# A load order and the transposes of two tiles at the start of a fused attention and MLP kernel: x tile 2 behind w1's third quarter, the transposes one group forward

## The chip, the cores and the metric

One core of a Trainium2 chip. The metric is the device time of one execution in microseconds (us), as a median of several. All runs told of here are of the fast or undisturbed kind; the granted clock of TensorE was 0.999 or 1.000 in every profile. TensorE is called PE, VectorE DVE, ScalarE ACT, GpSimd POOL, and SP is the queue that issues most loads. Tiles of x and groups of matmuls are counted from 0, the quarters of w1 from first to fourth.

## The reference, cut to what matters

The program adds three things: the input, a recurrent attention layer with memory tokens over the normalized input, and a mixer MLP over the normalized input. The first stage of the MLP:

```python
def _B_ref(x, w1, w2, w3, w4):        # x is already layernormed once
    h = _gelu(_layernorm(x, axis=-1) @ w1)      # x: 2048 x 1024, w1: 1024 x 1024
    # ... shifts by one and two tokens, w2, residual, second layernorm, w3, w4 ...
```

x is 2048 tokens of 1024 values, taken in 16 tiles of 128 tokens. w1 is 1024 x 1024.

## The kernel before

The whole kernel takes some 1510 us and PE is busy nearly all of them. The first 30 us are the start of the MLP: load x tiles and w1, normalize each tile (DVE and POOL), transpose it on PE against an identity, copy the transposed tile from PSUM to SBUF (ACT), multiply by w1 (PE), apply GELU (ACT). The loads are issued in this order on one queue:

```python
load_x(0)
for c in range(4):                     # w1 in four quarters of 512 KB
    nc.sync.dma_start(w1_sb[:, 2 * c:2 * c + 2, :], w1_v[:, 2 * c:2 * c + 2, :])
    if c < 2:
        load_x(1 + c)                  # an x tile is 256 KB
for n in range(3, 7):
    load_x(n)
# ... w2 in four parts, then load_x(7) to load_x(9) ...
```

The first tile is multiplied row block by row block, so that it can begin with the first quarter. The transposes of tile 1 stand ahead of the last two row blocks, which are the fourth quarter:

```python
def stage1_k(xn2T):
    # ...
    for k in range(KT):                # KT = 8; quarter c is k = 2c and 2c + 1
        if k == KT - 2:
            tr(1, 0)                   # four transposes each
            tr(1, 1)
        for co in range(KT):
            nc.tensor.matmul(pss[co // 4][:, co % 4, :], w1_sb[:, k, co * P:(co + 1) * P], xn2T[:, 0, k, :], # ...
```

Tiles 1 to 3 are multiplied group by group (eight output blocks `co`, each a group of eight matmuls over k). The transposes of the next tile lie between the groups that `between` names:

```python
def stage1(n0, nt, xn2T, between, j0=0):
    for co in range(KT):
        # ... eight matmuls, then GELU on ACT ...
        for f in between.get(co, ()):
            f()

for n in range(1, NPE):
    # ... statistics and normalization of tiles n and n + 1 on DVE ...
    if n == 1:
        stage1_k(tiles2[0])
    elif n < 4:
        stage1(n - 1, 1, tiles2[(n - 1) // 2 * 2], {7 - n: [lambda n=n: tr(n, 0)], 8 - n: [lambda n=n: tr(n, 1)]}, (n - 1) % 2)
```

Of the kernel before, what the change touches and what calls it, by code (L numbers as in the profile page):

```python
# [77 lines left out]
def kernel(  # L78
# [115 lines left out]
    with tc.manual_schedule(engines={mybir.EngineType.PE, mybir.EngineType.SP, mybir.EngineType.Pool}), ExitStack() as actx:  # L194
# [6 lines left out]
        with ExitStack() as bctx:  # L201
# [13 lines left out]
            with ExitStack() as hctx:  # L215
# [7 lines left out]
                with ExitStack() as p0:  # L223
# [7 lines left out]
                    def load_x(n):  # L231
                        if n < NT:
                            xts[n] = ring.tile([P, D], BF16, tag="xt", bufs=10, name=f"xt{n}")
                            nc.sync.dma_start(xts[n][:], x_v[:, n, :])

                    load_x(0)
                    for c in range(4):
                        nc.sync.dma_start(w1_sb[:, 2 * c:2 * c + 2, :], w1_v[:, 2 * c:2 * c + 2, :])
                        if c < 2:
                            load_x(1 + c)  # L240
                    for n in range(3, 7):
                        load_x(n)
                    for i in range(4):
# [6 lines left out]
                    def norm_stats(n, part=None):  # L250

                        if n >= NT:
                            return
                        xt = xts[n]
                        if n not in stats:
                            stats[n] = [ring.tile(shape, F32, tag=tag, bufs=6, name=f"{tag}{n}") for tag, shape in (("st", [P, 2, 6]), ("mv", [P, 2]), ("ab", [P, 2]), ("rr", [P, 2]), ("nm2", [P, 1]))]
                        st, mv, ab, rr, nm2 = stats[n]
                        if part in (None, 0):
                            nc.vector.bn_stats(st[:, 0, :], xt[:, 0:512])
                        if part == 0:  # L260
                            return
                        nc.vector.bn_stats(st[:, 1, :], xt[:, 512:1024])
                        nc.vector.bn_aggr(mv[:], st[:])
                        nc.vector.scalar_tensor_tensor(ab[:], epsm[:], mv[:, 1:2], epsa[:], op0=ALU.mult, op1=ALU.add)
                        nc.gpsimd.tensor_tensor(rr[:], ab[:], neghalf[:], op=ALU.pow)
                        if n >= NPE:
                            nc.gpsimd.tensor_scalar(nm2[:], mv[:, 0:1], rr[:, 1:2], -1.0, op0=ALU.mult, op1=ALU.mult)
# [12 lines left out]
                    def norm1(n):  # L280
                        st, mv, ab, rr, nm2 = stats[n]
                        xn = xn_keep[n // 4][:, n % 4]
                        nc.vector.tensor_scalar(xn, xts[n][:], mv[:, 0:1], rr[:, 0:1], op0=ALU.subtract, op1=ALU.mult)
                        nc.gpsimd.dma_start(xn_v[:, n, :], xn)
                        load_x(n + 10)
                        if n in (12, 15):
                            load_w3()
                        return xn

                    def transposes(xn2, xn2T, jj, half, halves=False):  # L290
                        ps = psum0.tile([P, 4, P], F32, tag="tr")
                        for k in range(4):
                            nc.tensor.matmul(ps[:, k, :], xn2[:, (half * 4 + k) * P:(half * 4 + k + 1) * P], ident[:], start=True, stop=True)
                        step = 2 if halves else 4
                        for i in range(0, 4, step):
                            nc.scalar.copy(xn2T[:, jj, half * 4 + i:half * 4 + i + step, :], ps[:, i:i + step])

                    def stage1_k(xn2T):

                        pss = [psum.tile([P, 4, P], F32, tag="mm", bufs=4, name=f"ps{i}") for i in range(2)]  # L300
                        for k in range(KT):
                            if k == KT - 2:
                                tr(1, 0)
                                tr(1, 1)
                            for co in range(KT):
                                nc.tensor.matmul(pss[co // 4][:, co % 4, :], w1_sb[:, k, co * P:(co + 1) * P], xn2T[:, 0, k, :],
                                                 start=(k == 0 and co % 4 == 0), stop=(k == KT - 1), skip_group_check=True)
                        for i in range(2):
                            nc.scalar.activation(hTB[:, 4 * i:4 * i + 4, 2:2 + P], pss[i][:], ACTF.Gelu_apprx_tanh)

                    def stage1(n0, nt, xn2T, between, j0=0):
                        w = nt * P
                        for co in range(KT):
                            ps = psum.tile([P, 512], F32, tag="mm", bufs=4)
                            for k in range(KT):
                                nc.tensor.matmul(ps[:, :w].rearrange("p (n t) -> p n t", t=P), w1_sb[:, k, co * P:(co + 1) * P],  # L316
                                                 xn2T[:, j0:j0 + nt, k, :], start=(k == 0), stop=(k == KT - 1))
                            nc.scalar.activation(hTB[:, co, 2 + n0 * P:2 + n0 * P + w], ps[:, :w], ACTF.Gelu_apprx_tanh)
                            for f in between.get(co, ()):
                                f()  # L320
# [13 lines left out]
                    tiles2, xn2s = {}, {}  # L334

                    def norm2_of(n):
                        if n % 2 == 0:
                            tiles2[n] = xn2T_tile()
                        xn2s[n] = norm2(n, tiles2[n - n % 2], n % 2)

                    def tr(n, half, halves=False):
                        transposes(xn2s[n], tiles2[n - n % 2], n % 2, half, halves)
# [9 lines left out]
                    for n in range(1, NPE):  # L352
                        if n > 1:
                            norm_stats(n + 1, 0)
                        norm2_of(n)
                        norm_stats(n + 1, 1 if n > 1 else None)
                        if n > 1:
                            norm1(n - 2)
                        if n == 1:
                            stage1_k(tiles2[0])  # L360
                        elif n < 4:
                            stage1(n - 1, 1, tiles2[(n - 1) // 2 * 2], {7 - n: [lambda n=n: tr(n, 0)], 8 - n: [lambda n=n: tr(n, 1)]}, (n - 1) % 2)
                    stage1(3, 1, tiles2[2], {0: [lambda: tr(4, 0)], 2: [lambda: tr(4, 1)], 4: [lambda: tr(5, 0)], 5: [lambda: tr(5, 1)]}, 1)

                    def prep(n):
# [44 lines left out]
            with ExitStack() as p3:  # L410
# [118 lines left out]
                for tb in range(4):  # L529
# [18 lines left out]
                    for j in range(4):  # L548
                        n = tb * 4 + j
# [462 lines left out]
```

## Time and profile before

| | before |
|---|---|
| median of the first three runs | 1510.9 us (1510.87 to 1511.14) |
| span of the profile | 1509.0 us |
| PE busy | 1499.1 us |
| w1's second, third, fourth quarter landed | 7.69, 9.67, 11.03 |
| PE starts the sixteen matmuls of the third and of the fourth quarter | 9.715, 11.08 |
| first transposes of tile 6, called **M** below | 26.40 |

How to read it: a time without a unit is us from the first instruction of the profiled execution. A transfer has landed when the last of its sixteen landing marks is in the trace (the profile counts 16 DMA engines). M is a milestone: all PE work of the changed stretch lies before it. "The last sixteen" are the matmuls of the first tile with w1's fourth quarter. The distance from the last sixteen to M tells what the moved transposes do, and the distance from the fourth quarter's landing to the last sixteen tells what the moved load does; in the profiles of the table further below neither depends on how late the loads were in one execution. The lines of this profile stand in the prediction.

### The profile page before, as it was taken

The numbers are of one execution on the slowest core, as the hardware profiler recorded it, in microseconds if no ns is written. First come the engines' busy times: TensorE is split into PE (matmuls) and PEld (weight loads), VectorE is DVE, ScalarE is ACT, GpSimd is POOL, SyncE is SP. The second block draws the span as 40 slices with busy tenths as digits, with TensorE's granted clock in tenths as the row PEclk, the third lists the DMA queues.
The fourth block names the chain that finished last, engine by engine and source line by source line (L and its number), as shares of the span: only waits on it lengthen the run. The fifth ranks groups of instructions, "written<-read, shape, count | busy, mean of one in ns | idle before, by whom it ended". The sixth has DMA issues, their size and how long they took to land.

```text
span 1509.0 us, 24273 instructions
## 1 busy us (share of the span) xinstructions
PE 1499.1 (99%) x9778; PEld 804.6 (53%) x9850; DVE 544.6 (36%) x1136; ACT 504.0 (33%) x1144; POOL 175.0 (12%) x245
## 2 busy tenths in 40 slices
PE   9999999999999999999999999999999999999998
PEld 8844444445444444444466645664665455545555
DVE  8382230100020212211246624651564166516641
ACT  6533103013012011111156614650663266416630
POOL 5241020211111221100000000001000100010001
PEclk9999999999999999999999999999999999999999
DMA  8699752363345877622389957992998299918921
GB/s 303 143 273 320 216 177 90 136 203 112 126 159 149 196 247 253 217 98 84 126 224 253 243 125 178 252 241 67 240 252 203 74 227 227 214 60 199 217 48 51
DMA packets 303251, 272.41 MB, mean 181 GB/s; under 512 B 153894, under 2 KB 270152, under 8 KB 303136
## 3 DMA queue, kind: packets, MB, share of 16 engines
q1 hardware_dynamic: 281248, 189.92, 51.1%
q0 software_dynamic: 21744, 80.83, 15.7%
q8 instruction: 79, 1.29, 0.4%
q14 instruction: 36, 0.29, 0.1%
q10 hardware_dynamic: 144, 0.07, 0.0%
HBM read 190.08 MB, written 45.29 MB: 156 GB/s over the span
## 4 chain that ended last, share of the span: by engine, by line
PE 98%; DMA 1%; issue 0%; SPq 0%; DVE 0%
PE ps L654 30%; PE pso L712 15%; PE ps L593 15%; PE ps L534 13%; PE ps L560 13%; PE ps L392 4%; PE ps L316 3%; PE psO L693 2%; PE psS L669 2%; PE ps L852 1%; PE ps L484 1%; DMA PT<-Pn 1%; PE gps L463 0%; PE ps L449 0%; DMA w_sb<-in_B_w_dram 0%
## 5 line engine op out<-in xcount | busy, mean ns | idle before, releaser
L654 PE MATMUL ps<-hTb,wt 128*128 128x396 bf16 (+2 forms) x2528 | 484.8, 342 | 0.0
L654 PEld LDWEIGHTS <-wt 128*128 128x128 bf16 x2528 | 236.8, 98 | 175.4
L593 PE MATMUL ps<-wt,xT 128*128 128x512 bf16 x1003 | 220.1, 379 | 1.1
L712 PE MATMUL pso<-wo_sb,oX 128*128 128x512 bf16 (+1 forms) x972 | 208.5, 372 | 1.1
L534 PE MATMUL ps<-xn3T,w_sb 128*128 128x512 bf16 x896 | 196.2, 379 | 0.0
L560 PE MATMUL ps<-w_sb,h3T 128*128 128x512 bf16 x873 | 194.3, 379 | 1.2
L593 PEld LDWEIGHTS <-xT 128*128 128x128 bf16 x1024 | 100.2, 98 | 120.8
L535 ACT ACTIVATE h3T<-ps 128x512 bf16<-128x512 f32 x112 | 66.8, 597 | 290.4 <-PE ps L534 289.5
L712 PEld LDWEIGHTS <-oX 128*128 128x128 bf16 x992 | 96.3, 98 | 107.4
L656 ACT CAST KT<-ps 128x462 bf16<-128x462 f32 (+2 forms) x160 | 81.7, 510 | 203.1 <-PE ps L654 199.0
L560 PEld LDWEIGHTS <-h3T 128*128 128x128 bf16 x896 | 87.0, 98 | 103.4
L534 PEld LDWEIGHTS <-w_sb 128*128 128x128 bf16 x896 | 86.6, 98 | 102.1
L675 DVE TENSOR_REDUCE sums<-sm 99x4 f32<-99x396 f32 (+2 forms) x176 | 97.6, 555 | 114.3 <-ACT sm L673 114.3
L658 ACT ACTIVATE QT<-ps 128x462 bf16<-128x462 f32 (+2 forms) x160 | 83.8, 524 | 120.4 <-PE ps L654 106.1
L595 ACT CAST Vs<-ps 128x512 bf16<-128x512 f32 x64 | 37.4, 585 | 233.2 <-PE ps L593 175.0
L671 DVE TENSOR_TENSOR sm<-psS,c_mask_reg_sb 99x396 f32<-99x396 f32 x152 | 86.7, 570 | 72.6 <-PE psS L669 72.4
L599 DVE CAST Vs<-ps 128x512 bf16<-128x512 f32 x64 | 44.3, 692 | 171.6 <-PE ps L593 163.2
L673 ACT ACTIVATE sm<-sm 99x396 f32<-99x396 f32 (+2 forms) x176 | 92.8, 527 | 34.7 <-DVE sm L671 27.9
L681 DVE TENSOR_TENSOR Pn<-sm,rs 99x396 bf16<-99x396 f32 (+2 forms) x176 | 98.9, 562 | 6.8 <-DMA PT<-Pn 0.9
L719 POOL DMA_DIRECT2D out_dram<-ot x30 | 16.4, 545 | 698.9 <-DVE ot L718 693.0
L561 DVE TENSOR_TENSOR R<-ps,R 128x512 f32<-128x512 f32 x32 | 21.9, 689 | 173.5 <-PE ps L560 156.8
L718 DVE TENSOR_TENSOR ot<-pso,Rt 128x512 bf16<-128x512 f32 (+1 forms) x33 | 22.2, 675 | 170.6 <-PE pso L712 166.5
(122 smaller groups left out, 1054.1 us busy)
## 6 DMA issues: line engine op xcount, KB each, us to landing
wt<-in_A_Wq_dram SPq DMA_DIRECT2D x76, 512.0 KB
wt<-in_A_Wk_dram SPq DMA_DIRECT2D x76, 512.0 KB
wt<-in_A_Wv_dram POOLq DMA_DIRECT2D x24, 1024.0 KB, 6.5
V_scratch<-Vs SPq DMA_DIRECT2D x32, 512.0 KB
V<-V_scratch SPq DMA_DIRECT2D x40, 384.0 KB
R_scratch<-x POOLq DMA_DIRECT2D x16, 512.0 KB, 3.5
R<-R_scratch SPq DMA_DIRECT2D x16, 512.0 KB
R_scratch<-R POOLq DMA_DIRECT2D x16, 512.0 KB, 3.1
```

Source lines behind the costliest of these rows:

```text
L534: nc.tensor.matmul(ps[:].rearrange("p (n t) -> p n t", t=P), w3_sb[:, k, f * P:(f + 1) * P], xn3T[tb][:, :, k, :], start=(k == 0), stop=(k ...
L535: nc.scalar.activation(h3T[:, f, :], ps[:], ACTF.Gelu_apprx_tanh)
L560: nc.tensor.matmul(ps[:], h3T[:, f, j * P:(j + 1) * P], w4_sb[:, f, ch * 512:(ch + 1) * 512], start=(f == 0), stop=(f == FT - 1))
L593: nc.tensor.matmul(ps[:], xT[:, m4 * 4 + j, k, :], wv[:, k, :], start=(k == 0), stop=(k == KT - 1))
L654: nc.tensor.matmul(ps[:, :nb], w[:, k, hh * P:(hh + 1) * P], B["hT"][:, k, :nb], start=(k == 0), stop=(k == KT - 1))
L656: nc.scalar.copy(dst[:, hh, :], ps[:, :nb])
L658: nc.scalar.mul(dst[:, hh, :], ps[:, :nb], scale)
L671: nc.vector.tensor_tensor(sm[:T, :, :T], S3, t["mask"][:].unsqueeze(1).to_broadcast((T, 4, T)), op=ALU.add)
L673: nc.scalar.activation(e[:T, :, :T], sm[:T, :, :T], ACTF.Exp, scale=LN2)
L675: nc.vector.tensor_reduce(ss, e[:T, :, :T], axis=AX.X, op=ALU.add)
L681: nc.vector.tensor_tensor(Pn[:T, :, :T], e[:T, :, :T], rs[:T, :].unsqueeze(2).to_broadcast((T, 4, T)), op=ALU.mult)
L712: nc.tensor.matmul(self.ps[:, :self.w], self.oX[0][:, h, self.oX[1] + self.gl * P:self.oX[1] + (self.gl + 1) * P], wo_sb[:, h, self.cc], s ...
```

## The change

Its intent: PE was seen to wait for w1's third quarter, so x tile 2, which is needed later, gives way to it; and the transposes of tiles 2 and 3 move one group of eight matmuls forward, so that their copies are done when the next tile begins. This is the whole diff:

```diff
                     for c in range(4):
                         nc.sync.dma_start(w1_sb[:, 2 * c:2 * c + 2, :], w1_v[:, 2 * c:2 * c + 2, :])
-                        if c < 2:
-                            load_x(1 + c)
+                        if c in (0, 2):
+                            load_x(1 + c // 2)
@@
                         elif n < 4:
-                            stage1(n - 1, 1, tiles2[(n - 1) // 2 * 2], {7 - n: [lambda n=n: tr(n, 0)], 8 - n: [lambda n=n: tr(n, 1)]}, (n - 1) % 2)
+                            stage1(n - 1, 1, tiles2[(n - 1) // 2 * 2], {6 - n: [lambda n=n: tr(n, 0)], 7 - n: [lambda n=n: tr(n, 1)]}, (n - 1) % 2)
```

## The prediction

> **What bounds the kernel now.** I read the page first, then the waits of the matmul engine, then the timeline of its first 20 us, then the load queue in the same stretch. The page gives the engine:
>
> ```profile
> span 1509.0 us, 24273 instructions
> PE 1499.1 (99%) x9778; PEld 804.6 (53%) x9850; DVE 544.6 (36%) x1136; ACT 504.0 (33%) x1144; POOL 175.0 (12%) x245
> PE 98%; DMA 1%; issue 0%; SPq 0%; DVE 0%
> ```
>
> The reader is to see that the matmul engine (PE) fills 1499 of 1509 us and 98% of the chain that ended last. The change adds and removes no instruction: the row counts of all five engines are equal in both kernels, and only the order of three stretches differs. So it can win only idle time of PE in the first 20 us. There is little. The waits of PE over the whole execution:
>
> ```profile
> PE warm L333 <- DVE wz L327: 1.4, 1, 1.4
> PE ps L306 <- DMA w_sb<-in_B_w_dram: 0.3, 1, 0.3
> PE ps L306 <- ACT xn2T L296: 0.2, 1, 0.2
> PE psO L693 <- DMA PT<-Pn: 0.2, 1, 0.2
> ```
>
> (Columns: who waited for what, us in total, times, longest.) L306 is the product of the first x tile with w1, row block k by row block k; a quarter of w1 is two blocks, sixteen matmuls. The second line is the target: PE waited once for w1. The timeline says when:
>
> ```profile
> 7.45 1.95 PE L306 MATMUL ps<-xn2T,w_sb 128*128 128x128 bf16 x32 [0.24 <-ACT xn2T L296]
> 9.71 1.07 PE L306 MATMUL ps<-xn2T,w_sb 128*128 128x128 bf16 x16 [0.32 <-DMA w_sb<-in_B_w_dram]
> 10.62 0.61 PE L293 MATMUL ps<-c_ident_sb,xn 128*128 128x128 bf16 x8
> 11.08 1.07 PE L306 MATMUL ps<-xn2T,w_sb 128*128 128x128 bf16 x16
> ```
>
> (Start, length, then the instructions; the bracket is the idle time before them and its releaser.) 32 matmuls use quarters one and two, 16 wait for the third, then the 8 transposes of tile 1, then 16 with the fourth quarter. From one start to the next, single records show 56 ns in a full stream, so without the wait the third quarter's matmuls would start at 7.453 + 32 x 0.056 = 9.24, not 9.715: 0.48 us lost (the view says 0.32, because it counts a matmul as busy for 219 ns).
>
> The load queue gives the landings, since an issue that needs a transfer's semaphore again starts just after that transfer landed:
>
> ```profile
> 8.34 0.38 SPq L244 DMA_DIRECT2D w_sb<-in_B_w_dram  x1
> 9.69 0.37 SPq L244 DMA_DIRECT2D w_sb<-in_B_w_dram  x1
> 11.05 0.37 SPq L244 DMA_DIRECT2D w_sb<-in_B_w_dram  x1
> 11.73 0.34 SPq L234 DMA_DIRECT2D xt<-in_A_x_dram  x1
> ```
>
> The landing marks in the trace (sixteen a transfer, I take the last) agree: w1's second quarter 7.69, x tile 2 8.32, third quarter 9.67, fourth quarter 11.03, x tile 3 11.71. An x tile (256 KB) takes 0.63 to 0.68 us of the stream, a quarter (512 KB) 1.35. **The fourth quarter lands at 11.03 and PE uses it at 11.08**, when its transposes happen to end as well, so no wait shows there: it is a hidden second gate.
>
> A smaller stall stands in no list, because it lies under the listing's threshold. The chain of waits cuts PE's run exactly there:
>
> ```profile
> 15.72 0.67 PE ps L316 x12
> 16.39 0.00 issue
> 16.39 2.17 PE ps L316 x36
> ```
>
> and so does the timeline of ScalarE (ACT):
>
> ```profile
> 15.09 0.58 ACT L296 CAST xn2T<-ps 128x512 bf16<-128x512 f32 x1
> 15.57 0.28 ACT L318 ACTIVATE hTB<-ps 128x128 bf16<-128x128 f32 x1
> 15.76 0.58 ACT L296 CAST xn2T<-ps 128x512 bf16<-128x512 f32 x1
> ```
>
> L316 is the product of tiles 1 and later, eight groups of eight matmuls each. The 12 are the last group of tile 1 and k 0 to 3 of tile 2's first group. The next matmul needs the second half of tile 2's transposed copy, which ends at 15.76 + 0.58 = 16.34. Single records: a start at 16.171, the next at 16.394, 223 ns instead of 56. It is no lost record: exactly 36 matmuls follow up to tile 3's transposes at 18.40, 4 of the first group and 4 groups of 8. So 0.167 us are lost.
>
> **What the Trainium skill says.** "Perfetto Trace Analysis", Optimization Strategy: find the gaps on the contended engine and what semaphore ends each. That is what I do, with the caution that a gap closed may hide a second semaphore. "DMA: Bandwidth & Descriptors", Queues, rings and completion order: on each DMA engine the descriptors of one queue are consumed in ring order, though completion between transfers is not strictly first in, first out. The trace agrees on order: the four landings above follow the issue order. So swapping two transfers swaps their places, and what follows both lands when it did. "TensorE: Matmul & The Clock Gate", Back-to-back issue gap, gives N/2.4 + 2.5 ns for isolated matmuls, 55.8 for N = 128, and about 81 for streams with weight loads; this trace has weight loads beside every matmul and still shows 56, which I use.
>
> **The change part by part.**
> 1. Third w1 quarter ahead of x tile 2. It starts when the second has landed, 7.69, and takes 1.35: it lands at about 9.04 (estimate from the landings above). PE then needs no wait and starts the third quarter's matmuls at 9.24 instead of 9.715. Locally -0.48 us.
> 2. Tile 1's transposes follow at 9.24 + 16 x 0.056 = 10.14. Their input is normalized by VectorE (DVE) from 9.21 to 9.76, so they can run there, and end at 10.14 + 8 x 0.056 = 10.59.
> 3. The fourth quarter. The same bytes lie ahead of it: it lands at 11.03 as before. PE is ready at 10.59, waits to about 11.08, and starts where it started before. The 0.48 us of step 1 come back as a wait of about 0.48. Sum of steps 1 to 3: 0.00, give or take 0.05.
> 4. x tile 2 lands at about 9.67 instead of 8.32. DVE took its statistics up at 9.67, after tile 1's normalization; now at 9.7. The few hundredths are absorbed: the next step, on GpSimd (POOL), starts at 11.55 because POOL issues loads until then, and DVE's next statistics wait for x tile 3 until 11.73 as before. Cost 0.
> 5. Tile 2's transposes one product group sooner, after groups 4 and 5 of tile 1. A group is 8 x 0.056 = 0.447 us; the copies end 0.447 sooner, the second at about 15.89. PE wants it at 16.004 + 4 x 0.056 = 16.23: ready with 0.3 to spare. Gain 0.167 us. Its input must be there at 14.66 - 0.447 = 14.21; DVE makes it from 12.35 to 12.88, so it is.
> 6. Tile 3's transposes one group sooner, after groups 3 and 4 of tile 2. Before, no step over 75 ns shows where tile 3 starts: gain 0. Its input is ready at 15.57, PE asks at about 17.6: no cost.
>
> Sum: 0.00 - 0.17 = -0.17 us, 0.01% of the time. PE runs without a visible wait up to 797 us, so this should reach the end: 1510.9 - 0.17 = **1510.7 us**.
>
> **The rivals.**
> (a) The gain of step 1 stays: then about -0.65 in all, 1510.3. It needs the fourth quarter to land sooner than 11.03. For it: the list of waits shows none for that quarter. Against: it lands 0.05 before its use, and the bytes ahead of it are unchanged.
> (b) Only the load order acts, and step 5 gives nothing (ACT late for another reason, or the 0.167 absorbed later): 1510.9. One later wait, for the transposed probabilities at 797 us (0.2 us, last of the waits of PE above), depends on DVE and DMA and could take it up or add its own scatter.
> (c) x tile 2, last in line, delays DVE and with it the transposes: +0.1 to +0.5, up to 1511.4. It speaks for it that the slack at 9.67 is nearly nil; against it that steps 4 to 6 leave 1.3 us at the transposes, after two fixed waits.
> (d) PE slows at a lower clock after the new idle time: the trace shows an idle stretch of like length at 9.24 before, with 56 ns before and after it, so I give it almost nothing.
>
> **Range and chances.** The three runs before spread over 0.27 us, as much as the whole effect. From (a), 1510.3, to (c)'s usual size, 1511.0, with 0.1 to 0.2 of scatter on each side, gives 1510.2 to 1511.2. 2% would be 30 us, more than all idle time of PE (10 us), so faster or slower by that is out but for an accident: 0.005 each.
>
> **What would show it.** Step 1: no idle time before the third quarter's sixteen matmuls, which start near 9.24. Step 3: a wait of PE for w1 before the last sixteen, which start at 11.05 to 11.12. Step 4: tile 2's statistics near 9.7, its normalization still at 12.35. Step 5: no cut at 16.39, and all later PE work of the stage about 0.17 sooner. I am wrong if the last sixteen start clearly before 11.0 (rival a), if tile 2's transposes wait for DVE (rival c), or if the stage ends sooner and the kernel doesn't (rival b).

## The result, and the profile after

Six runs of each kernel in the same series: **1511.01 us** with the change (1510.90 to 1511.43), **1511.02 us** before (1510.82 to 1512.17; its first three runs are among them). The ratio is 0.9999, 95% interval 0.9986 to 1.0011: the same. A ratio here compares the fast runs of both kernels in the same rounds and is not quite the ratio of the two medians.

The profile of the changed kernel looked odd at first. Its waits of PE, as who waited for what, us in total, times and longest, cut to one line; and its timeline (start, length, instructions; idle time before them and its releaser in brackets):

```profile
PE ps L306 <- DMA w_sb<-in_B_w_dram: 1.0, 3, 0.5
```

```profile
7.40 1.05 PE L306 MATMUL ps<-xn2T,w_sb 128*128 128x128 bf16 x16
8.64 1.07 PE L306 MATMUL ps<-xn2T,w_sb 128*128 128x128 bf16 x16 [0.19 <-DMA w_sb<-in_B_w_dram]
10.00 1.07 PE L306 MATMUL ps<-xn2T,w_sb 128*128 128x128 bf16 x16 [0.29 <-DMA w_sb<-in_B_w_dram]
10.90 0.61 PE L293 MATMUL ps<-c_ident_sb,xn 128*128 128x128 bf16 x8
12.03 1.07 PE L306 MATMUL ps<-xn2T,w_sb 128*128 128x128 bf16 x16 [0.52 <-DMA w_sb<-in_B_w_dram]
```

Three waits for w1 stand where there was one, and the last sixteen start at 12.03 instead of 11.08. The new wait ahead of them was predicted. The other two come from late landings: the second quarter landed at 8.60 instead of 7.69, though the four transfers up to it are issued in the same order in both kernels. The marks show where the delay is: the sixteen marks of the fourth quarter run from 10.64 to 11.98 here, and from 10.48 to 11.03 in the profile before, so a part of the transfer lagged; why it did stays open. The lag began early: the last mark of w1's first quarter was at 6.06, against 5.19 in the profile before. At M this execution was 0.79 us behind the one before (27.19 against 26.40), at its end only 0.28 (span 1509.3 against 1509.0). The rest was regained at two places far from the change, 0.38 near 797 and 0.13 near 1389, where products with transposed probabilities started late in the profile before and not in this one (in the list of waits of this profile that line is gone).

So one profile on each side can't tell the change from the luck of the execution. The experiments compare the two distances instead, over many executions.

### The profile page after: what moved, and what is told of

Same layout as the page of the kernel before. It is cut to its first block, busy times and chain, and to the rows that moved or that the text cites. A ratio compares the mean times of both kernels' runs of the same rounds, so it can differ in the third digit from the quotient of the medians.

```text
span 1509.3 us, 24345 instructions
## 1 busy us (share of the span) xinstructions
PE 1502.8 (100%) x9850; PEld 804.6 (53%) x9850; DVE 545.0 (36%) x1136; ACT 504.6 (33%) x1144; POOL 175.4 (12%) x245
## 4 chain that ended last, share of the span: by engine, by line
PE 99%; DMA 1%; SPq 0%; DVE 0%; issue 0%
PE ps L654 30%; PE pso L712 15%; PE ps L593 15%; PE ps L534 13%; PE ps L560 13%; PE ps L392 4%; PE ps L316 3%; PE psS L669 2%; PE psO L693 2%; PE ps L852 1%; PE ps L484 1%; DMA w_sb<-in_B_w_dram 1%; PE gps L463 0%; PE ps L449 0%; PE ps L293 0%; SPq L234 0%
```

## The experiments

**The theories.** Mine (C): the reordered load gains nothing, since the fourth quarter, which lands when it did, is a second gate (a transfer that PE would have had to wait for next); the moved transposes gain 0.17 us; late landings and late waits are chance. Rivals: (O) the new order itself makes the early landings late; (G) the removed wait is a gain that the end gets; (A) the copy of tile 2 is late for another reason than the place of its transposes; (L) later waits take up what the start gains.

### The changed kernel again, twice

No edit. For the first repeat:

> The changed kernel once more. In its first profile w1's second quarter landed at 8.60 instead of 7.69 and the fourth at 11.98 instead of 11.03. Theory C (chance: one DMA engine lagged in that one execution, whatever the load order): here the second quarter lands anywhere from 7.6 to 8.7, and PE's last sixteen products with the first tile start within 0.1 us of the fourth quarter's landing. Rival O (the new order itself makes the early landings late): second quarter again at about 8.6, last sixteen again at about 12.0. Time: C and O both within 0.5 us of before; M, the first transposes of tile 6 (26.40 before, 27.19 in the first profile of the change), comes 15.16 us after the last sixteen under both, against 15.32 before.

Measured: ratio 1.0002 (0.9988 to 1.0015), median 1511.55 us. In this execution the second quarter landed at 7.54 (a little sooner than C's 7.6 to 8.7, and far from O's 8.6), the third at 9.03, the fourth at 11.05. The timeline of PE:

```profile
7.47 2.84 PE L306 MATMUL ps<-xn2T,w_sb 128*128 128x128 bf16 x48
10.14 0.61 PE L293 MATMUL ps<-c_ident_sb,xn 128*128 128x128 bf16 x8
11.10 1.07 PE L306 MATMUL ps<-xn2T,w_sb 128*128 128x128 bf16 x16 [0.34 <-DMA w_sb<-in_B_w_dram]
```

This is the undisturbed picture of the change. 48 matmuls run in one piece: the wait for the third quarter is gone, and its first matmul started at 9.25. The transposes are done near 10.59, and then PE waits for the fourth quarter: the step from one start to the next is 564 ns in place of 56, so 0.51 us are lost, about as much as was lost before (0.48). The last sixteen start 0.05 after the landing, at the time when they started before. The chain of waits of the same run, where the piece of tile 1's last group meets tile 2's first:

```profile
15.07 0.22 PE ps L293 x4
15.29 2.68 PE ps L316 x48
```

Before, the chain was cut into 12 and 36 matmuls with a break of 0.167 us; now the 48 are one piece. M comes 15.157 after the last sixteen, against 15.321.

For the second repeat:

> The changed kernel a third time. Theory: PE starts the last sixteen 0.04 to 0.06 us after the fourth quarter's landing, with the transposes of tile 1 done 0.3 to 0.6 before; M 15.15 to 15.16 after the last sixteen, as in its two profiles so far. The fourth quarter lands anywhere from 10.8 to 12. Ratio of the time 0.9999 within 0.0005. Rival: in some execution the fourth quarter is early enough that the removed wait becomes a gain, last sixteen at 10.6.

Measured: ratio 0.9999 (0.9985 to 1.0013), median 1510.81 us. The fourth quarter landed at 11.64, the last sixteen started at 11.684, M 15.158 later. The wait in front of the last sixteen is there in all three profiles of the change; the fourth quarter was never early enough to leave a gain.

### The load order alone

```diff
-                        if c < 2:
-                            load_x(1 + c)
+                        if c in (0, 2):
+                            load_x(1 + c // 2)
```

> Only the load order changed, transposes as before. Theory (the fourth quarter is a second gate): no gain that lasts; PE waits for the fourth quarter after tile 1's transposes, the last sixteen start 0.05 after that landing, M comes 15.32 us after the last sixteen as before, with the 223 ns step before tile 2's fifth matmul. Time ratio 1.0000 within 0.0003. Rival (the removed wait is a gain): last sixteen 0.4 us sooner relative to the third quarter's landing than before (1.37 us before), and time 0.4 us shorter.

Measured: ratio 1.0001 (0.9987 to 1.0014), median 1511.26 us. The timeline of PE:

```profile
7.65 2.88 PE L306 MATMUL ps<-xn2T,w_sb 128*128 128x128 bf16 x48 [0.21 <-ACT xn2T L296]
10.38 0.61 PE L293 MATMUL ps<-c_ident_sb,xn 128*128 128x128 bf16 x8
11.45 1.07 PE L306 MATMUL ps<-xn2T,w_sb 128*128 128x128 bf16 x16 [0.47 <-DMA w_sb<-in_B_w_dram]
```

The wait has moved from the third quarter to the fourth, and the last sixteen start 0.04 after that one's landing (11.41). The chain is cut as in the kernel before:

```profile
16.09 0.67 PE ps L316 x12
16.76 0.00 issue
16.77 2.17 PE ps L316 x36
```

M comes 15.321 after the last sixteen, as before to the nanosecond. My expectation also gave rival G a sign that was badly chosen: the last sixteen relative to the third quarter's landing. It was 2.03, longer and not shorter than before, but it grows by itself when the third quarter comes sooner, so it doesn't measure a gain. The distance to the fourth quarter's landing decides: PE had finished its transposes and stood waiting for that landing, which is against G.

### The transposes alone

```diff
-                            stage1(n - 1, 1, tiles2[(n - 1) // 2 * 2], {7 - n: [lambda n=n: tr(n, 0)], 8 - n: [lambda n=n: tr(n, 1)]}, (n - 1) % 2)
+                            stage1(n - 1, 1, tiles2[(n - 1) // 2 * 2], {6 - n: [lambda n=n: tr(n, 0)], 7 - n: [lambda n=n: tr(n, 1)]}, (n - 1) % 2)
```

> Only the transposes of tiles 2 and 3 moved, loads as before. Theory: the whole local gain of the change is here: no step over 75 ns where tile 2's fifth product starts, M 15.15 to 15.17 us after the last sixteen (15.32 before). Time: at best 0.17 us shorter, not to be told from the scatter of the runs (0.3 us and more). Rival: the copy was late for another reason, so the step of 223 ns stays and M stays 15.32 after.

Measured: ratio 1.0000 (0.9987 to 1.0014), median 1511.48 us. The timeline of PE shows the old wait for the third quarter and none for the fourth:

```profile
9.53 1.07 PE L306 MATMUL ps<-xn2T,w_sb 128*128 128x128 bf16 x16 [0.26 <-DMA w_sb<-in_B_w_dram]
10.43 0.61 PE L293 MATMUL ps<-c_ident_sb,xn 128*128 128x128 bf16 x8
10.88 1.06 PE L306 MATMUL ps<-xn2T,w_sb 128*128 128x128 bf16 x16
```

The chain of waits has one piece where the kernel before has 12 and 36:

```profile
14.84 0.22 PE ps L293 x4
15.06 2.68 PE ps L316 x48
```

M comes 15.146 after the last sixteen, 0.175 sooner than before, and the break of 223 ns is gone. (Some 0.01 of the 0.175 lies in the last sixteen themselves: their second step is 56 ns here and 66 where PE had waited for them.) So the local gain of the change is all here, and rival A falls.

### The kernel before again

No edit.

> The kernel before, profiled and timed once more. Theory C (early landings and late waits differ from execution to execution, whatever the load order): w1's fourth quarter lands between 10.6 and 12.0 and PE's last sixteen start about 0.05 after it or when tile 1's transposes end, whichever is later; M (first transposes of tile 6) 15.32 after them, with the step of 223 ns. Rival O (this load order lands early, the changed one late): fourth quarter at 10.8 to 11.1, as in the two profiles with this order, against 11.05 to 12.0 with the changed one. Ratio of the time 1.0000 within 0.0005, and the runs spread over 1 us or more.

Measured: ratio 0.9999 (0.9985 to 1.0012), median 1511.47 us. The fourth quarter landed at 11.45, later than the 10.8 to 11.1 that rival O asks for, and M came 15.320 after the last sixteen. The spread of 1 us or more that I expected was not in these five runs (1511.38 to 1511.66); it was in the nine of the same rounds (1510.63 to 1512.67).

### One x tile more ahead of the fourth quarter

```diff
                         if c < 2:
                             load_x(1 + c)
-                    for n in range(3, 7):
+                        if c == 2:
+                            load_x(3)
+                    for n in range(4, 7):
```

> The kernel before with x tile 3 moved ahead of w1's fourth quarter, nothing else. Theory (the fourth quarter is the second gate): it lands 0.65 to 0.7 us later, 2.0 after the third quarter in place of 1.36, and PE, which then waits for it, starts the last sixteen 2.0 after the third quarter's landing; M as far behind as before, 15.32; time +0.65 us if it reaches the end, ratio 1.0004. Rival (the fourth quarter has slack): last sixteen 1.37 after the third quarter's landing, as before.

Measured: ratio 1.0010 (0.9996 to 1.0023), median 1512.30 us; the wide scatter (1511.64 to 1515.74) leaves the time unclear. The trace is clear (this kernel is two lines longer, so L306 is called L308 here, and L293 L295):

```profile
10.68 1.07 PE L308 MATMUL ps<-xn2T,w_sb 128*128 128x128 bf16 x16 [0.97 <-DMA w_sb<-in_B_w_dram]
11.59 0.61 PE L295 MATMUL ps<-c_ident_sb,xn 128*128 128x128 bf16 x8
12.73 1.07 PE L308 MATMUL ps<-xn2T,w_sb 128*128 128x128 bf16 x16 [0.53 <-DMA w_sb<-in_B_w_dram]
```

The fourth quarter landed at 12.68, 2.04 after the third (10.64) in place of 1.36, and the last sixteen followed at once, 0.05 later; M came 15.321 after them, as before. With nothing else changed, delaying the fourth quarter delays the stage: it was the second gate in the kernel before too, hidden because PE was ready in the same moment. That was no luck of one execution: after the third quarter PE has 24 steps of 56 ns to do, 1.34 us, and in the four profiles with the old order the fourth quarter landed 1.34 to 1.37 after the third. The step onto the last sixteen shows who came last: 70, 70, 59 and 56 ns in these four (before, before again, the delay, transposes alone), so in three of them PE did wait, by 3 to 14 ns, which no listing shows.

### A known delay

```diff
+                    ps = psum.tile([P, 512], F32, tag="mm", bufs=4, name="delay")
+                    for i in range(10):
+                        nc.tensor.matmul(ps[:], wz[:, :P], wz[:], start=(i == 0), stop=(i == 9))
                     stage1(3, 1, tiles2[2], ...
```

> The kernel before with ten dummy products of 512 columns put in on PE ahead of tile 3's product (nobody reads them): a known delay of 10 x 0.216 = 2.16 us on PE at about 20 us. Theory (PE's early time reaches the end nearly whole): time 1.7 to 2.3 us longer than before, ratio 1.0011 to 1.0015. Rival (later waits take up early differences): under 1 us longer. M comes 17.4 to 17.5 after the last sixteen in place of 15.32.

Measured: M comes 17.478 after the last sixteen, 2.16 more than before, as intended. Median 1513.93 us against 1511.89 in the same rounds, so 2.04 more; ratio 1.0016 (1.0003 to 1.0030, which is 0.5 to 4.5 us). The fastest of these five runs (1513.58) is 0.9 above the slowest of the nine before. So a delay of 2 us gets to the end in the main, and rival L falls for that size; for 0.17 us it stays open. In the first profile of the change 0.51 of 0.79 us was regained, but no such absorption shows in general: from M to the end the three profiles of the changed kernel took 1482.06 to 1482.45 us and the two of the kernel before 1482.57 and 1482.90. That scatter is itself larger than 0.17.

### Beyond the change: x tile 2 behind all of w1

If the fourth quarter is the second gate, it has to come sooner too.

```diff
                             # as the change, but:
-                        if c in (0, 2):
-                            load_x(1 + c // 2)
+                        if c in (0, 3):
+                            load_x(1 + c // 3)
```

> As the change, but x tile 2 is loaded behind all four quarters of w1. Theory (the fourth quarter is the second gate): it lands one tile sooner, 0.65 us, so PE's last sixteen start when the transposes of tile 1 end, with no wait or a wait under 0.2 us if the early landings are not late; against the second quarter's landing the last sixteen start 2.9 to 3.0 us later in place of 3.4. M about 15.16 after the last sixteen unless x tile 2 delays tile 2's transposes. Time 0.4 to 0.6 us shorter than before if early gains last to the end, ratio 0.9996 to 0.9997. Rival (x tile 2 is what then delays): the last sixteen start sooner, but tile 2's transposes wait for its normalization, M over 15.4 after, and time not shorter.

Measured: ratio 1.0002 (0.9988 to 1.0015), median 1511.68 us. The timeline of PE:

```profile
7.36 2.84 PE L306 MATMUL ps<-xn2T,w_sb 128*128 128x128 bf16 x48
10.04 0.61 PE L293 MATMUL ps<-c_ident_sb,xn 128*128 128x128 bf16 x8
10.49 1.06 PE L306 MATMUL ps<-xn2T,w_sb 128*128 128x128 bf16 x16
```

The fourth quarter landed at 9.98, no wait is left in front of the last sixteen, and they start at 10.49. (I had reckoned 2.9 to 3.0 after the second quarter's landing; it was 3.2.) Both gates are open. But my time, 0.4 to 0.6 us shorter, did not come, and the rival of this expectation did. The late x tile takes part of the gain back: tile 2's transposes wait 0.31 us for its normalization (M comes 15.465 after the last sixteen), and 0.23 us more are lost near 32.7, where tile 6's product waits for a copy that stands on ACT behind the late normalization of tile 8.

The same with the transposes where they were before the change:

```diff
-  ... {6 - n: [lambda n=n: tr(n, 0)], 7 - n: [lambda n=n: tr(n, 1)]}, (n - 1) % 2)
+  ... {7 - n: [lambda n=n: tr(n, 0)], 8 - n: [lambda n=n: tr(n, 1)]}, (n - 1) % 2)
```

> x tile 2 behind all quarters of w1, as in the earlier run, with the transposes of tiles 2 and 3 where they were before the change. There tile 2's transposes waited 0.31 us for its normalization. Theory: asked for 0.45 us later they wait for nothing, but the copy of their second half is late again, 0.167 us; sum 0.14 better than that run up to tile 3. Whether the later stall near 32.7 (0.23 us, tile 6 waits for its copy behind a normalization on ACT) stays is open: it comes from the late x tile 2 through DVE and POOL, so I expect it here as well. Time within 0.4 us of before.

Measured: ratio 0.9994 (0.9981 to 1.0008), median 1510.46 us. M came 15.311 after the last sixteen, 0.154 better than with the earlier transposes, where I expected 0.14; the break of 223 ns was back, and so was the stall near 32.8. The runs were further below before (0.0006, 0.9 us) than the 0.4 that I had allowed. To see whether 0.9994 was real, once more:

> Once more the version whose ratio was 0.9994 with five runs. Theory: at M it is 0.4 us ahead of before, then 0.25 us are lost near 32.8, so the time is 0.2 us shorter on average, ratio 0.9998 to 1.0000; the 0.9994 was mostly scatter. Rival: it is really 0.6 to 1.0 us shorter, ratio 0.9993 to 0.9996 again.

Measured: ratio 1.0003 (0.9990 to 1.0017), median 1511.86 us. The 0.9994 was scatter. Here the loads were later (second quarter at 8.04), tile 2's transposes waited 0.29 for their input even at their old place, and M came 15.612 after the last sixteen, at 26.44, so the lead of 0.4 at M that I expected was not there.

Last, all three stalls at once: both halves of tile 2's transposes behind group 5, and the preparation of tiles 8 and 9 later, so that ACT copies first.

```diff
                             # x tile 2 behind all quarters, and:
-  ... {7 - n: [lambda n=n: tr(n, 0)], 8 - n: [lambda n=n: tr(n, 1)]}, (n - 1) % 2)
+  ... {5: [lambda: tr(2, 0), lambda: tr(2, 1)]} if n == 2 else {4: [lambda: tr(3, 0)], 5: [lambda: tr(3, 1)]}, (n - 1) % 2)
@@
-                            between[1 + 2 * (n0 == 4)] += [lambda n0=n0: prep(n0 + 4)]
-                            between[4 + 2 * (n0 == 4)] += [lambda n0=n0: prep(n0 + 5)]
+                            between[1 + 5 * (n0 == 4)] += [lambda n0=n0: prep(n0 + 4)]
+                            between[4 + 3 * (n0 == 4)] += [lambda n0=n0: prep(n0 + 5)]
```

> x tile 2 behind all quarters of w1; both halves of tile 2's transposes after group 5 of tile 1 (late enough for their input, early enough for the copy); the preparation of tiles 8 and 9 moved behind groups 6 and 7 of the tile 4 and 5 product, so that ACT copies tile 6 and 7 before it normalizes tile 8. Theory: all three stalls found so far go: last sixteen start with no wait, M 15.15 after them, no step over 130 ns near 32.8. About 0.4 + 0.17 us sooner than before at M in an undisturbed start; time 0.5 to 0.8 us shorter, ratio 0.9995 to 0.9997, at the edge of what the scatter lets one see. Rival: a later preparation delays tile 8's product, which shows as a step near 39.7.

Measured: ratio 0.9995 (0.9981 to 1.0009), median 1510.25 us, all five runs within 1510.19 to 1510.52. In the profile M was 0.61 us sooner than before (25.79) and no stall stood near 32.8 or 39.7; M came 15.356 after the last sixteen, since tile 2's transposes still waited 0.13 for their input. It looked like a version that beats both. Repeated:

> The best version once more, to see whether its gain repeats, since another version's 0.9994 did not. Its five runs gave 1510.19 to 1510.52, on average 0.82 us under the runs of before in the same rounds. Theory (0.6 us at the first transposes of tile 6, no stall near 32.8, and some luck in the late waits): mean 0.4 to 0.9 us under before, ratio 0.9994 to 0.9997, no wait of PE for w1, last sixteen when tile 1's transposes end. Rival (scatter): ratio 0.9999 to 1.0003, with the same early trace.

Measured: ratio 0.9998 (0.9985 to 1.0012), median 1511.46 us. The theory of the expectation (0.9994 to 0.9997) fell, and its rival (0.9999 to 1.0003 with the same early trace) did not hold either: the ratio lies between the two, and the early trace was not the same. This profile was taken in an execution with late loads:

```profile
9.80 1.07 PE L306 MATMUL ps<-xn2T,w_sb 128*128 128x128 bf16 x16 [0.29 <-DMA w_sb<-in_B_w_dram]
10.70 0.61 PE L293 MATMUL ps<-c_ident_sb,xn 128*128 128x128 bf16 x8
11.15 1.06 PE L306 MATMUL ps<-xn2T,w_sb 128*128 128x128 bf16 x16
12.05 2.84 PE L316 MATMUL ps<-xn2T,w_sb 128*128 128x128 bf16 x48
15.04 0.62 PE L293 MATMUL ps<-c_ident_sb,xn 128*128 128x128 bf16 x8
```

The second quarter landed at 8.39 and the third at 9.75, x tile 2 only at 11.79, and its normalization held up its transposes by 0.31 (15.04 in place of 14.73). In such an execution even this version waits at the start, and M came at 26.70. So I found no version that beats both in every execution; its mean over ten runs is 1510.82 us, and its gain is not shown.

### What the executions have in common

| profile | third quarter landed | its matmuls start | fourth quarter landed | last sixteen start | M after them |
|---|---|---|---|---|---|
| before | 9.67 | 9.715 | 11.03 | 11.080 | 15.321 |
| before again | 10.08 | 10.127 | 11.45 | 11.492 | 15.320 |
| transposes alone | 9.48 | 9.530 | 10.82 | 10.880 | 15.146 |
| order alone | 9.43 | 9.472 | 11.41 | 11.453 | 15.321 |
| changed, first | 9.95 | 9.997 | 11.98 | 12.030 | 15.157 |
| changed, second | 9.03 | 9.250 | 11.05 | 11.098 | 15.157 |
| changed, third | 9.61 | 9.654 | 11.64 | 11.684 | 15.158 |

Read the last columns. The last sixteen start 0.04 to 0.06 after the fourth quarter's landing under either load order, and that landing is about 2.0 after the third quarter's with the x tile between them and 1.34 to 1.37 without: the transfers only trade places. (The last number of a row is the distance from the last sixteen to M.) M after them is 15.32 with the old transposes and 15.15 to 15.16 with the new. Where the fourth quarter lands differs from execution to execution by 0.75 us under the old order (with the delayed kernel's 11.57) and by 0.93 under the new, four to six times what the transposes gain.

On rival O: with the old order (the three above and the delayed kernel, 11.57) the fourth quarter landed at 10.82 to 11.57, with the new one at 11.05 to 11.98. The two overlap over most of their width. A small effect of the order on these landings is not excluded by four profiles a side, but the second quarter, at 7.42 to 8.20 and at 7.54 to 8.60, shows a like scatter with nothing reordered ahead of it; in the run with x tile 3 ahead, whose order up to there is the old one, it landed at 8.60 as well. And in the five profiles with x tile 2 behind all of w1, where the third quarter follows the second directly as in the change, it landed at 7.28, 7.37, 7.37, 8.04 and 8.39. That the differences are chance is read from this scatter, not shown by a cause.

## Why the prediction was right, point by point

The measured 1511.01 lies in the range of 1510.2 to 1511.2, and "within 2%" was right. But that range also holds the times of rivals (a), 1510.3, and (b), 1510.9, so the time alone could not tell the mechanism; only the traces could. Its steps:

1. Third quarter. Foretold: landing 9.04, its matmuls at 9.24. In the undisturbed execution 9.03 and 9.25. In the two with late loads a shorter wait stayed there.
2. Tile 1's transposes from 10.14: measured 10.14.
3. Fourth quarter. Foretold: lands as before, a new wait of about 0.48, last sixteen at 11.08, net 0.00. Measured 11.05, 0.51 and 11.10. The load order alone confirmed it, and the run with x tile 3 ahead showed the same gate from the other side. The prediction's reading that the quarter lands "0.05 before its use" was too kind: where PE openly waited for a quarter, its first matmul started 0.045 to 0.047 after the landing too, so nothing was to spare. This is the step that decided: the diff promises half a microsecond, and a transfer that the diff doesn't touch takes it back.
4. x tile 2 later. Its statistics began at 9.85 and its normalization at 12.50 in the undisturbed execution, both some 0.15 later than I wrote, because tile 1's normalization was later there by as much; the transposes came at 14.23, so it cost nothing. With x tile 2 one place later still it did cost 0.31.
5. Tile 2's transposes. Foretold: -0.167. Measured 0.163 to 0.175 in the three profiles of the change and that of the transposes alone.
6. Tile 3's transposes. Foretold: 0. The distances to M leave no room for anything beside step 5. (They came at 17.81 in the undisturbed execution, not at about 17.6: the old 18.40 less a group of 0.447 and the 0.167 is 17.79, so that sum was off by 0.2, without effect.)

**The sum** of -0.17 is confirmed at M. At the end of the kernel it can't be seen in any one series. Over the three series in which both kernels ran, 16 runs of the changed kernel average 1511.13 us and 24 of the one before 1511.20, a difference of 0.07 with a standard error of 0.16: neither 0.17 nor 0 can be told from that. (The two other series, without the changed kernel, ran on other chips and gave 1511.79 and 1511.55 for the nine runs of the kernel before in each; mixing them in would turn 0.07 into an apparent 0.28.) So a gain at the end of the kernel is not shown.

**What was too small was the scatter.** I took the spread of three runs, 0.27 us, for the noise. In all, the 47 runs of the kernel before reach from 1510.18 to 1512.67. Two sources of it are seen in the traces: how late the last landing marks of the first loads are, and the waits of PE for the transposed probabilities near 797 and 1389, which the list of waits gives with up to 0.4 us each and which were missing in some executions. Rival (b) named the second; the first was not among my rivals. A range of 1510.2 to 1511.2 for a median of six held this time, but the medians of the same changed kernel in its other two series were 1511.55 and 1510.81, so it was narrower than the data allow, and that it held was partly luck.

Of the rivals, (a), a gain at the fourth quarter, was seen in none of the four profiles with that order. (c), a delay through x tile 2, was not seen with the change and was seen when the tile went one place further back. (d), a slower PE after the new idle time, was not seen: the steps after the wait are 56 ns, but for the first (67 ns).

## What to carry to other kernels

Before moving a transfer ahead to close a gap, find the landing of the next transfer in line and the time at which its user will then be ready: bytes that swapped places here left the later landing where it was, and a gate at which PE waited for only 14 ns showed up in no list of waits. Judge a change of tenths of a microsecond by distances between events in the trace (landing to first use, first use to a milestone), repeated over a few executions; here these were constant to some hundredths from execution to execution, while total times scattered over more than 2 us. Breaks shorter than the listing's threshold can be found where the chain of waits cuts a run of equal instructions in two.

## What the Trainium skill lacked or had wrong

- "TensorE: Matmul & The Clock Gate", Back-to-back issue gap: for streams with weight loads it gives about 81 ns for a matmul of 128 columns and 131 ns for 512. Here, with a weight load beside each matmul, starts lay 56 ns apart at 128 columns and 109 ns at 256; ten products of 512 columns, the delay experiment, took 2.16 us, 216 ns each. The page's formula for isolated matmuls (N/2.4 + 2.5 ns) fits all three.
- "DMA: Bandwidth & Descriptors", Queues, rings and completion order, says that completion is not first in, first out, but gives no size for how far the DMA engines of one transfer drift apart. In one execution the sixteen marks of one 512 KB load spread over 1.34 us (10.64 to 11.98), in another over 0.55 (10.48 to 11.03), and PE, where it waited for a quarter, started 0.045 to 0.047 after the last mark.
- "Perfetto Trace Analysis", Optimization Strategy, says to find the gaps and the semaphore that ends each. It doesn't warn of a semaphore whose wait is too short to show as a gap: the step onto the fourth quarter's matmuls was 70 ns in place of 56, and once the gap of 0.48 us ahead of it was closed, the wait there grew to 0.51.
